# Three spaced value pairs a chunk by seven products, in a form with the signs turned, and turned tiles in four shared buffers

## The chip, the cores and the metric

The kernel runs on one core of one Trainium2 chip. The metric is the time of one execution in device microseconds (us); lower is better. The engines are PE (TensorE: matmuls), DVE (VectorE), ACT (ScalarE), POOL (GpSimd) and SP (SyncE, which here only issues transfers).

## The reference

The input is a batch of 8 with 8 heads of 1024 tokens and a head width of 64. Keys and values are projected along the sequence from 1024 to 64 rows, then attention runs over these 64, and its output goes through a gated feed-forward layer.

```python
k_proj = np.einsum('ks,bhsd->bhkd', E, k)
v_proj = np.einsum('ks,bhsd->bhkd', F, v)
scores = scale * np.matmul(q, k_proj.transpose(0, 1, 3, 2))
scores = scores - np.max(scores, axis=-1, keepdims=True)
attn = np.exp(scores)
attn = attn / (np.sum(attn, axis=-1, keepdims=True) + 1e-09)
attn_out = np.matmul(attn, v_proj)
x = attn_out.transpose(0, 2, 1, 3).reshape(B * S, H * D)      # 8192 x 512
g = x @ w_gate                                                # 512 x 1536
silu = g * (1.0 / (1.0 + np.exp(-g)))
val = x @ w_val                                               # 512 x 1536
out = silu * val @ w_out                                      # 8192 x 512
```

## The kernel before

All matmuls take bf16 inputs and sum in fp32 in PSUM. The work is cut into 16 chunks of 512 tokens, two a batch: chunk c is half c % 2 of batch c // 2. A chunk's feed-forward part has 12 blocks f of 128 columns of the hidden layer. Time is counted in steps t = 12 c + f, and every step has two slots, 2t and 2t + 1, for pieces of attention.

One step of the main loop issues, in this order: the gate matmuls of block f (`f_g`, four matmuls of 512 columns, then SiLU on ACT), the attention pieces of slot 2t, the value matmuls (`f_v`, four matmuls, then the product with the SiLU on DVE into `hT`), the list `late[t]`, and the pieces of slot 2t + 1. Everything is issued in the written order, and each engine works through its own queue in that order; semaphores hold an instruction until its inputs are there and its output buffer is free.

`late` holds the rest. `f_m(c, n)` is the output product of the chunk before. It is a 2 x 2 block product by seven products instead of eight (n runs over 14 pieces of six matmuls of 256 columns; `m_34`, `m_52`, `m_16` and `m_7` read the sums out of PSUM on ACT, POOL and DVE). `h_sum` makes the sums of quarters of `hT` that it needs: m = 1, 6, 7 on DVE in blocks 1 to 3 of the next chunk, m = 2, 5 on POOL, block by block.

The same idea is used for some value blocks. `PAIRED` says which: blocks 8 and 9 in chunks 3 to 14, blocks 10 and 11 in chunks 2 to 14. The two blocks of a pair, halved in the contraction and in the tokens, are a 2 x 2 product; seven products of two matmuls of 256 columns each take the place of two blocks of four matmuls of 512. `p_w` makes the sums of weights once, `p_x` the sums of a chunk's `xT` (67, 1, 3, 4), on POOL in even chunks and on DVE in odd ones. `f_v_pair` runs the products into two PSUM banks and puts the four outputs together on DVE.

The attention of batch b runs while the two chunks of batch b - 1 are in the feed-forward part; `place(b)` puts its pieces into slots, counted from s0 = 48 (b - 1): `u_KV` (projections; slot 8), `u_KT` (turns the projected keys, four casts by DVE into `BD`; slot 11), `u_S` (scores and exponential; slots 13, 13, 15, 15 in the even chunk, 25, 25, 27, 27 in the odd one), `u_R` and `u_N` (softmax sum with reciprocal on DVE, product on POOL), `u_AD` (SP turns the attention weights by a transposing DMA), `u_PVt` (values; four casts by ACT into `xT`). `u_TD` turns q by the same kind of DMA.

PSUM has eight banks: two for gates, two for values (`vps`, taken in turn), two for the output product, two for attention. The turned tiles (`qTd`, `AAd`, `AT`) have two buffers each.

Of the kernel before, what the change touches and what calls it, by code (L numbers as in the profile page):

```python
# [16 lines left out]
H = 8  # L17
# [21 lines left out]
PAIRED = {8: range(3, NC - 1), 10: range(2, NC - 1)}  # L39
# [4 lines left out]
def kernel(  # L44
# [34 lines left out]
    ps_v = ctx.enter_context(tc.tile_pool(name="psv", bufs=2, space=bass.MemoryType.PSUM))  # L79
# [18 lines left out]
    wo = w_pool.tile([P, NFT, DM], BF16, name="wo")  # L98
    ws = {m: w_pool.tile([P, HF, HC], BF16, name=f"ws{m}") for m in (1, 3, 4, 6, 7)}
# [57 lines left out]
    banks = {"a": (ps_a, "pa"), "g": (ps_g, "gps"), "v": (ps_v, "vps"), "y": (ps_y, "yp0"), "z": (ps_y, "yp1")}  # L157
    ring = {"n": 0, "wide": True}

    def bank(where, shape, dt, name):  # L160
        if where == "a" and ring["wide"]:
            where = "aaz"[ring["n"] % 3]
            ring["n"] += 1
        pool, tag = banks[where]
        return pool.tile(shape, dt, name=name, tag=tag)
# [179 lines left out]
    def u_TD(b, ch):  # L345

        t = aw.tile([P, 2 * H, P], BF16, name="qTd", tag="qTd")
        nc.sync.dma_start_transpose(
            out=t[:], in_=qb[b, ch][:].rearrange("p h j d -> p (h j d)")
        )  # L350
        qT[b, ch, "d"] = t

    def u_AD(b, ch):
        t = aw.tile([P, 4, NPAIR, P], BF16, name="AT", tag="AT")
        nc.sync.dma_start_transpose(
            out=t[:].rearrange("p j a t -> p (j a) t"),
            in_=AA.pop((b, ch, "d"))[:].rearrange("p j h k -> p (j h k)"),
        )
        AT[b, ch] = t
# [45 lines left out]
    def u_N(b, u, eng=nc.gpsimd):  # L405
        ch, w = divmod(u, 4)
        g, i = divmod(w, 2)
        if (b, ch) in by_dma:
            if (b, ch, "d") not in AA:
                AA[b, ch, "d"] = aw.tile([P, 4, H, KP], BF16, name="AAd", tag="AAd")  # L410
            a = AA[b, ch, "d"][:, 2 * i : 2 * i + 2, 4 * g : 4 * g + 4, :]
        else:
            a = AA[b, u] = first_batch("a", [P, 2, 4, KP], "AA")
            a = a[:]
        zr, r = rr.pop((b, u))
        eng.tensor_tensor(  # L416
            out=a.rearrange("p j h k -> p h j k"),
            in0=ee.pop((b, u))[:],
            in1=r.unsqueeze(3).to_broadcast([P, 4, 2, KP]),
            op=ALU.mult,  # L420
        )
        if maxed:
            return
        unwatched.append(zr)
        if b or u > 3:
            u_Z()
# [8 lines left out]
    def u_A(b, u, eng=nc.vector):  # L435
        ch, w = divmod(u, 4)
        g, i = divmod(w, 2)
        if (b, ch) not in AT:
            AT[b, ch] = aw.tile([P, 4, NPAIR, P], BF16, name="AT", tag="AT")
        ps = bank("a", [P, 2, 2, P], BF16, "aTp")  # L440
        a = AA.pop((b, u))
        for pr in range(2):
            for j in range(2):
                nc.tensor.transpose(
                    out=ps[:, j, pr, :],
                    in_=a[:, j, 2 * pr : 2 * pr + 2, :].rearrange("p h k -> p (h k)"),
                    identity=ident_bf[:],
                )
        copy(eng, AT[b, ch][:, 2 * i : 2 * i + 2, 2 * g : 2 * g + 2, :], ps[:])
# [88 lines left out]
    def paired(c, f):  # L538
        return not maxed and c in PAIRED.get(f - f % 2, ())

    def f_g(c, f, i=None):
        ps = f_mm(c, f, 0, i)
        if paired(c, f):
            if f % 2 == 0:
                pool, tag = {8: (q_pool, "q01"), 10: (fw, "thp")}[f]
                gp["p"] = pool.tile([P, 2, CW], FP32, name="thp", tag=tag, bufs=1)
            nc.scalar.activation(out=gp["p"][:, f % 2], in_=ps[:], func=AF.Silu)  # L547
            return
# [10 lines left out]
    def p_tiles():  # L559


        a = q_pool.tile([P, 8, HT], BF16, name="xsa", tag="q00", bufs=1)
        rows = [quarter(wo, 0, 1)[:, i] for i in range(4)] + [quarter(wo, 1, 0)[:, i] for i in range(HF)]
        for m, x in ((6, a[:, 0:2]), (7, a[:, 2:4]), (67, a[:, 0:4]), (1, a[:, 4:6]), (3, a[:, 6:8])):
            sums["x", m] = x
        sums["x", 4] = quarter(wo, 0, 1)[:, 4:6]
        for i, m in enumerate((1, 2, 5, 6, 7)):
            for n, f in enumerate((8, 10)):
                sums["w", m, f] = rows[5 * n + i].rearrange("p (k t) -> p k t", k=2)

    def p_w(m, f):

        p = f
        f = [slice(i * P, (i + 1) * P) for i in (p, p + 1)]
        a = {(i, j): wv[:, 2 * j : 2 * j + 2, f[i]] for i in range(2) for j in range(2)}
        x, y, op = {
            1: ((0, 0), (1, 1), ALU.add),
            2: ((1, 0), (1, 1), ALU.add),
            5: ((0, 0), (0, 1), ALU.add),
            6: ((1, 0), (0, 0), ALU.subtract),  # L580
            7: ((0, 1), (1, 1), ALU.subtract),
        }[m]
        nc.vector.tensor_tensor(out=sums["w", m, p], in0=a[x], in1=a[y], op=op)

    def p_x(c, m, eng):

        if not sums:
            p_tiles()
        x = xT[divmod(c, CH)]
# [3 lines left out]
            1: (b[0, 0], b[1, 1], ALU.add),  # L593
            3: (b[0, 1], b[1, 1], ALU.subtract),
            4: (b[1, 0], b[0, 0], ALU.subtract),
        }[m]
        eng.tensor_tensor(out=sums["x", m], in0=i0, in1=i1, op=op)  # L597

    def p_mm(c, p, m, ps, start=False):
# [4 lines left out]
        xs = {2: x[:, 0:2, 0:HT], 5: x[:, 2:4, HT:CW]}[m] if m in (2, 5) else sums["x", m]  # L604
# [10 lines left out]
    def f_v_pair(c, f):  # L615

        tensor_tensor = nc.vector.tensor_tensor
        p = f - f % 2
        if f == p:
            xp = gp["x"] = bank("v", [P, 2, HT], FP32, "vps")  # L620
            t = gp["t"] = fw.tile([P, 2, HT], FP32, name="vt", tag="s1", bufs=1)
            p_mm(c, p, 3, xp[:, 0], start=True)
            p_mm(c, p, 4, xp[:, 1])
            copy(nc.scalar if (c + f // 2) % 2 else nc.vector, t[:, 0], xp[:, 0])
            tensor_tensor(out=t[:, 0], in0=t[:, 0], in1=xp[:, 1], op=ALU.add)
            zp = gp["z"] = bank("v", [P, 2, HT], FP32, "vps")
            p_mm(c, p, 1, zp[:, 0], start=True)
            tensor_tensor(out=t[:, 1], in0=t[:, 0], in1=zp[:, 0], op=ALU.add)
            return
        th, xp, zp, t = (gp.pop(i) for i in "pxzt")  # L630
        th = th[:].rearrange("p i t -> p (i t)")
        h = hT[c][:, p : p + 2, :].rearrange("p i t -> p (i t)")
        p_mm(c, p, 5, xp[:, 0])
        p_mm(c, p, 2, xp[:, 1])
        tensor_tensor(out=t[:], in0=t[:], in1=xp[:], op=ALU.subtract)
        tensor_tensor(
            out=h[:, HT : 3 * HT], in0=th[:, HT : 3 * HT], in1=xp[:].rearrange("p i t -> p (i t)"), op=ALU.mult
        )
        p_mm(c, p, 6, zp[:, 1])
        p_mm(c, p, 7, zp[:, 0])  # L640
        tensor_tensor(out=t[:], in0=t[:], in1=zp[:], op=ALU.add)
        h, th = (a.rearrange("p (i t) -> p i t", i=4)[:, 0::3] for a in (h, th))
        tensor_tensor(out=h, in0=th, in1=t[:], op=ALU.mult)

    def f_v(c, f, i=None):
        if paired(c, f):
            return f_v_pair(c, f)
# [55 lines left out]
    def h_sum(c, m, f0, f1, eng=nc.gpsimd):  # L703

        if f0 == 0:
            if c == NC - 1 and m in (1, 6, 7):

                pool, tag = {1: (kv_pool, "vb"), 6: (kv_pool, "kb"), 7: (aw, "AAd")}[m]
                hs[c, m] = pool.tile([P, HF, HT], BF16, name=f"hs{m}", tag=tag)
# [125 lines left out]
    def put(s, fn, *a):  # L835
        slots[s].append((fn, a))

    def place(b):
# [11 lines left out]
        else:  # L850
# [8 lines left out]
            put(s0 + 28, u_AD, b, 0)  # L859
            put(s0 + 38, u_AD, b, 1)  # L860
            put(s0 + 44, u_PVt, b, 0, (0, 1), ("aa", "yz"))
        for j in range(NJ):
            put(sa[j], u_S, b, j)
            at = sa[j] + 1 if b == 1 else s0 + (
                (16, 17, 20, 21) if b == 2 else (14, 15, 17, 23)) [j] if j < 4 else s0 + (26, 28, 33, 35)[j - 4]
# [55 lines left out]
    with tc.manual_schedule():  # L921

        kb[0] = kv_pool.tile([P, H, NJ, D], BF16, name="kb", tag="kb")
        kraw = [aw.tile([P, 2, NJ * D], FP32, name="kraw", tag=tag) for tag in ("qTd", "AAd")]
# [148 lines left out]
        for c in range(1, NC):  # L1073
            for f in range(HF):
                for m in (5, 2):
                    at = {2: 10, 3: 11, 4: NFT, 5: NFT}[f] if paired(c, HF + f) else HF + f
                    late[c * NFT + at].append((h_sum, c, m, f, f + 1))
            if c == NC - 1:
                late[c * NFT + HF].append((h_sum, c, 6, 0, HF, nc.vector))
# [9 lines left out]
        for p, at in ((10, (3, 3, 3, 4, 4)), (8, (4, 4, 7, 7, 7))):  # L1089
            for i, f in zip((1, 2, 5, 6, 7), at):  # L1090
                late[2 * NFT + f].append((p_w, i, p))
        for c in PAIRED[10]:
            for i, m in enumerate((67, 1, 3, 4) if c % 2 == 0 else (3, 4, 1, 67)):
                f, eng = ((2, 3, 3, 5)[i], nc.gpsimd) if c % 2 == 0 else (6 + i // 2, nc.vector)
                late[c * NFT + f].append((p_x, c, m, eng))
# [3 lines left out]
        for t in range(NIT):  # L1099
# [3 lines left out]
            f_g(c, f, i)  # L1103
            run_slot(2 * t)
# [38 lines left out]
```

## Time and profile before

| | us |
|---|---|
| median of 3 runs | 544.71 (544.64 to 544.86) |
| profiled execution | 544.77 |
| its span | 543.1 |
| PE busy | 534.0 (98%) |
| DVE busy | 406.6 (75%) |
| POOL busy | 362.7 (67%) |
| ACT busy | 265.9 (49%) |
| two steady chunks (350.81 to 415.06) | 64.25, PE busy throughout |

Busy time of PE is modelled at the matmuls' ends, so it says that PE has no gaps, not that it works at its peak. The granted clock is 0.999 of full speed. A step of a steady chunk takes between 2.4 and 4 us on PE, by the attention pieces in it. The chain that ended last, followed back from the end, shows what set the time; a group's line may be that of a helper (L168 is `copy`).

### The profile page before, as it was taken

The page shows a single profiled execution, that of the slowest core. Times are in us where ns is not written, and L with a number is a line of the kernel's source. Part 1 is how long each engine was busy: PE and PEld are TensorE (multiplying, and loading weights), DVE is VectorE, ACT ScalarE, POOL GpSimd, SP SyncE. Part 2 cuts the span into 40 slices and gives each one's busy share as a digit, 9 for nine tenths or more (in the row PEclk, how much of TensorE's full clock was granted, in tenths as well). Part 3 has the DMA queues.
Part 4 walks back from the last instruction along what each step waited for, and adds up shares of the span by engine and source line. Part 5 has one row for each costly group of instructions (what it writes and reads, how often), then busy time and mean ns, then how long its engine had stood idle before and what let it go on. Part 6 is the DMA issues. An engine that isn't in the chain of part 4 may idle for free.

```text
span 543.1 us, 9860 instructions
## 1 busy us (share of the span) xinstructions
PE 534.0 (98%) x3708; PEld 328.3 (60%) x3708; DVE 406.6 (75%) x692; ACT 265.9 (49%) x454; POOL 362.7 (67%) x456
## 2 busy tenths in 40 slices
PE   8999999999999999999999999999999999999996
PEld 4654445565656666576665756566665766656665
DVE  3787897868768887689776897778975887757553
ACT  3565454564446634466335554465444663443331
POOL 6962398578466795669675694856956686565272
PEclk9999999999999999999999999999999999999999
DMA  9999969929941499007991099512992023100103
GB/s 200 191 196 200 162 145 192 180 63 150 198 96 41 98 214 192 8 34 132 215 158 40 3 198 185 122 40 63 190 185 69 39 80 78 40 39 4 43 34 121
DMA packets 112228, 62.94 MB, mean 116 GB/s; under 512 B 65968, under 2 KB 103856, under 8 KB 112176
## 3 DMA queue, kind: packets, MB, share of 16 engines
q0 software_dynamic: 43952, 29.49, 38.2%
q1 hardware_dynamic: 67392, 31.46, 25.9%
q10 hardware_dynamic: 832, 1.31, 0.8%
q8 instruction: 30, 0.49, 0.4%
q14 instruction: 22, 0.18, 0.1%
HBM read 60.29 MB, written 16.78 MB: 142 GB/s over the span
## 4 chain that ended last, share of the span: by engine, by line
PE 93%; DMA 2%; ACT 2%; POOL 1%; DVE 1%; issue 1%; POOLq 0%; ACTq 0%; DVEq 0%
PE gps L529 30%; PE yps L737 25%; PE vps L529 23%; PE vps L606 7%; PE sc L371 2%; DMA wv<-in_moe_w_val_dram 2%; PE kvp L180 2%; PE yps L671 2%; PE pv L475 1%; POOL vb L121 0%; ACT ee L379 0%; ACT xT L484 0%; POOL qb L133 0%; ACT L554 0%; ACT ysb L761 0%
## 5 line engine op out<-in xcount | busy, mean ns | idle before, releaser
L529 PE MATMUL gps<-xT,wg 128*128 128x512 bf16 (+1 forms) x772 | 196.6, 377 | 0.0
L529 PE MATMUL vps<-xT,wv 128*128 128x512 bf16 (+1 forms) x576 | 146.3, 377 | 1.1 <-DMA wv<-in_moe_w_val_dram 0.9
L720 POOL TENSOR_TENSOR hs<-hT 128x256 bf16<-128x256 bf16 x180 | 124.2, 718 | 23.1 <-DVE hT L653 21.8
L554 ACT ACTIVATE th<-gps 128x512 f32<-128x512 f32 x106 | 63.3, 597 | 136.4 <-PE gps L529 129.5
L529 PEld LDWEIGHTS <-wg 128*128 128x128 bf16 x776 | 74.0, 98 | 51.7 <-issue 0.5
L653 DVE TENSOR_TENSOR hT<-th,vps 128x512 bf16<-128x512 f32 x106 | 71.9, 679 | 43.1 <-PE vps L529 39.9
L737 PEld LDWEIGHTS <-hs 128*128 128x128 bf16 x900 | 87.9, 98 | 24.7 <-issue 0.6
L767 POOL TENSOR_TENSOR tt<-tt,ysb 128x512 f32<-128x512 f32 x28 | 35.6, 1271 | 91.0 <-DVE tt L766 90.5
L529 PEld LDWEIGHTS <-wv 128*128 128x128 bf16 x576 | 55.0, 98 | 67.1 <-issue 3.8
L416 POOL TENSOR_TENSOR AAd<-ee,zr 128x512 bf16<-128x512 f32 x56 | 59.9, 1070 | 30.1 <-ACT ee L379 17.8
L737 PE MATMUL yps<-ws,hs 128*128 128x256 bf16 x540 | 68.6, 273 | 0.2 <-DVE ysb L806 0.2
L720 DVE TENSOR_TENSOR hs<-hT 128x1536 bf16<-128x1536 bf16 (+1 forms) x49 | 65.1, 1334 | 0.1
L401 DVE TENSOR_REDUCE zr<-ee 128x8 f32<-128x512 f32 x64 | 43.3, 677 | 11.5 <-ACT ee L379 11.5
L737 PE MATMUL yps<-ws,hT 128*128 128x256 bf16 x360 | 48.8, 273 | 0.0
L737 PE MATMUL yps<-wo,hs 128*128 128x256 bf16 x360 | 48.6, 273 | 0.1
L737 PEld LDWEIGHTS <-hT 128*128 128x128 bf16 x360 | 35.2, 98 | 16.0
L547 ACT ACTIVATE thp<-gps 128x512 f32<-128x512 f32 x50 | 29.5, 597 | 31.2 <-PE gps L529 31.1
L597 POOL TENSOR_TENSOR xsa<-xT 128x512 bf16<-128x512 bf16 (+1 forms) x21 | 40.4, 1951 | 0.0
L379 ACT ACTIVATE ee<-sc 128x512 f32<-128x512 f32 x64 | 35.7, 607 | 4.3 <-PE sc L371 2.9
L756 POOL TENSOR_TENSOR tt<-xs 128x256 f32<-128x256 f32 x30 | 24.7, 824 | 16.5 <-ACT xs L754 16.5
L761 ACT COPY ysb<-yps 128x512 f32<-128x512 f32 x30 | 17.6, 585 | 27.0 <-PE yps L737 26.3
L754 ACT COPY xs<-yps 128x512 f32<-128x512 f32 x30 | 17.7, 590 | 25.3 <-PE yps L737 24.1
(133 smaller groups left out, 677.9 us busy)
## 6 DMA issues: line engine op xcount, KB each, us to landing
out_dram<-ysb SPq DMA_DIRECT2D x27, 512.0 KB, 2.8
qb<-in_q_dram POOLq DMA_DIRECT2D x14, 512.0 KB, 16.7
kb<-in_k_dram POOLq DMA_DIRECT2D x7, 1024.0 KB, 11.2
vb<-in_v_dram POOLq DMA_DIRECT2D x7, 1024.0 KB, 13.4
wo<-in_moe_w_out_dram POOLq DMA_DIRECT2D x2, 768.0 KB, 21.3
out_dram<-ysb SPq DMA_DIRECT2D x6, 256.0 KB, 2.4
kraw<-in_k_dram ACTq DMA_DIRECT2D x2, 512.0 KB, 4.7
qb<-in_q_dram POOLq DMA_DIRECT2D x4, 256.0 KB, 8.0
```

Source lines behind the costliest of these rows:

```text
L379: nc.scalar.activation(out=e[:].rearrange("p h j k -> p (h j k)"), in_=ps[:].rearrange("p a k -> p (a k)"), func=AF.Exp, scale=scale,)
L401: nc.vector.reduce_sum(out=z, in_=e[:], axis=AX.X)
L416: eng.tensor_tensor(out=a.rearrange("p j h k -> p h j k"), in0=ee.pop((b, u))[:], in1=r.unsqueeze(3).to_broadcast([P, 4, 2, KP]), op=ALU.mult,
L529: nc.tensor.matmul(out=ps[:, ts], lhsT=(wg, wv)[w][:, kt, f * P : (f + 1) * P], rhs=x[:, kt, ts], start=(kt == 0), stop=(kt == NKT - 1),)
L547: nc.scalar.activation(out=gp["p"][:, f % 2], in_=ps[:], func=AF.Silu)
L554: nc.scalar.activation(out=th[:], in_=ps[:], func=AF.Silu)
L597: eng.tensor_tensor(out=sums["x", m], in0=i0, in1=i1, op=op)
L606: nc.tensor.matmul(out=ps, lhsT=w[:, kt], rhs=xs[:, kt], start=(start and kt == 0), stop=(kt == 1), skip_group_check=True,)
L653: nc.vector.tensor_tensor(out=hT[c][:, f, :], in0=th[:], in1=ps[:], op=ALU.mult)
L720: eng.tensor_tensor(out=hs[c, m][:, fs, :], in0=quarter(hT[c], *a)[:, fs], in1=quarter(hT[c], *b)[:, fs], op=op,)
L737: nc.tensor.matmul(out=ps, lhsT=lhsT, rhs=ws[m][:, f, :] if rhs is None else rhs, start=(start and f == 0), stop=(f == HF - 1), skip_group ...
L767: nc.gpsimd.tensor_tensor(out=t[:], in0=t[:], in1=yo[c, p][:, 1:3], op=ALU.subtract)
```

## The change

Pairs are now blocks 2 and 3 (chunks 4 to 15), 5 and 6 (3 to 15), 8 and 9 (3 to 14); a plain block stands between them (blocks 4, 7, 10). The seven products are written with other signs, in four steps spread over three blocks: `p_34` and `p_1` in the first block, `p_52` in the second, `p_76` ahead of the value matmuls of the third. Products 4, 3, then 5, 2, then 7, 6 go to one PSUM bank, M1 to the other, and each bank has a name of its own (`v` takes the next one, `w` the other). ACT copies products 4 and 3 and M1 out of PSUM; DVE sums with the bank and multiplies with the SiLU in a separate step (`p_sum`, `p_h`), both inputs of `p_h` in SBUF. The SiLU of a pair's first block is issued behind that copy. M1 is added last.

All `p_x` sums are on DVE, in two sets of buffers by the parity of the chunk, and are made ahead: for an odd chunk in blocks 5 and 9 of the even chunk before, for an even one in block 11 of the chunk before and in block 0. There are five more sums of weights.

`qTd`, `AAd`, `AT` (and the first loads of k) share four rotating buffers. The slots of `u_AD` go from 28 and 38 to 29 and 42, those of `u_R` and `u_N` from 14, 15, 17, 23, 26, 28, 33, 35 to 16, 18, 20, 22, 31, 33, 36, 38 (b > 2). The POOL sums of `hT` stand at other steps.

```diff
-PAIRED = {8: range(3, NC - 1), 10: range(2, NC - 1)}
+PAIRED = {2: range(4, NC), 5: range(3, NC), 8: range(3, NC - 1)}
...
-    ps_v = ctx.enter_context(tc.tile_pool(name="psv", bufs=2, space=bass.MemoryType.PSUM))
+    ps_v = ctx.enter_context(tc.tile_pool(name="psv", bufs=1, space=bass.MemoryType.PSUM))
...
+        if where == "v":
+            v_turn[0] ^= 1
         pool, tag = banks[where]
+        if where in "vw":
+            tag += str(v_turn[0] ^ (where == "w"))
...
-        t = aw.tile([P, 2 * H, P], BF16, name="qTd", tag="qTd")
+        t = aw.tile([P, 2 * H, P], BF16, name="qTd", tag="turned", bufs=4)
...
-        t = aw.tile([P, 4, NPAIR, P], BF16, name="AT", tag="AT")
+        t = aw.tile([P, 4, NPAIR, P], BF16, name="AT", tag="turned", bufs=4)
...
-                AA[b, ch, "d"] = aw.tile([P, 4, H, KP], BF16, name="AAd", tag="AAd")
+                AA[b, ch, "d"] = aw.tile([P, 4, H, KP], BF16, name="AAd", tag="turned", bufs=4)
...
+    def paired(c, f):
+        p = 3 * ((f + 1) // 3) - 1
+        return p if not maxed and c in PAIRED.get(p, ()) and f < p + 2 else None
 
     def f_g(c, f, i=None):
         ps = f_mm(c, f, 0, i)
+        p = paired(c, f)
+        if p is not None:
+            if f == p:
+                gp["g"] = ps
+            else:
+                nc.scalar.activation(out=gp["p"][:, 1], in_=ps[:], func=AF.Silu)
             return
...
+    def p_sum(out, a, b, op):
+        nc.vector.tensor_tensor(out=out, in0=a.unsqueeze(1).to_broadcast([P, 2, HT]), in1=b, op=op)
+
+    def p_h(c, p, part, v):
+        h, th = (
+            a.rearrange("p i t -> p (i t)").rearrange("p (i t) -> p i t", i=4)[:, part]
+            for a in (hT[c][:, p : p + 2, :], gp["p"][:])
+        )
+        nc.vector.tensor_tensor(out=h, in0=th, in1=v, op=ALU.mult)
+
+    def p_34(c, p):
+        x = gp["x"] = bank("v", [P, 2, HT], FP32, "vps")
+        gp["m"] = bank("w", [P, 2, HT], FP32, "vps")
+        p_mm(c, p, 4, x[:, 0], start=True)
+        p_mm(c, p, 3, x[:, 1])
...
+        nc.scalar.copy(out=sx[:], in_=x[:])
+        gp["p"] = fw.tile([P, 2, CW], FP32, name="thp", tag="thp", bufs=1)
+        nc.scalar.activation(out=gp["p"][:, 0], in_=gp.pop("g")[:], func=AF.Silu)
+        nc.vector.tensor_tensor(out=ts[:, 0], in0=sx[:, 0], in1=sx[:, 1], op=ALU.add)
+
+    def p_1(c, p):
+        m = gp.pop("m")
+        p_mm(c, p, 1, m[:, 0], start=True)
+        nc.scalar.copy(out=gp["ts"][:, 1], in_=m[:, 0])
+
+    def p_52(c, p):
+        x, sx = gp["x"], gp["sx"]
+        p_mm(c, p, 5, x[:, 0])
+        p_mm(c, p, 2, x[:, 1])
+        p_sum(sx[:], gp["ts"][:, 0], x[:], ALU.subtract)
+        p_h(c, p, slice(1, 3), sx[:])
+
+    def p_76(c, p):
+        x, sx = gp.pop("x"), gp.pop("sx")
+        p_mm(c, p, 7, x[:, 0])
+        p_mm(c, p, 6, x[:, 1])
+        p_sum(sx[:], gp.pop("ts")[:, 1], x[:], ALU.add)
+        p_h(c, p, slice(0, 4, 3), sx[:])
+        gp.pop("p")
...
-            put(s0 + 28, u_AD, b, 0)
-            put(s0 + 38, u_AD, b, 1)
+            put(s0 + 29, u_AD, b, 0)
+            put(s0 + 42, u_AD, b, 1)
...
-                (16, 17, 20, 21) if b == 2 else (14, 15, 17, 23)) [j] if j < 4 else s0 + (26, 28, 33, 35)[j - 4]
+                16, 17 + (b > 2), 20, 22, 31, 33, 36, 38)[j]
...
-                    at = {2: 10, 3: 11, 4: NFT, 5: NFT}[f] if paired(c, HF + f) else HF + f
+                    at = (8, 7, 11, 11, 10, 11)[f] if c > 2 else HF + f
...
-        for p, at in ((10, (3, 3, 3, 4, 4)), (8, (4, 4, 7, 7, 7))):
-            for i, f in zip((1, 2, 5, 6, 7), at):
-                late[2 * NFT + f].append((p_w, i, p))
-        for c in PAIRED[10]:
-            for i, m in enumerate((67, 1, 3, 4) if c % 2 == 0 else (3, 4, 1, 67)):
-                f, eng = ((2, 3, 3, 5)[i], nc.gpsimd) if c % 2 == 0 else (6 + i // 2, nc.vector)
-                late[c * NFT + f].append((p_x, c, m, eng))
+        for p, ts in ((5, (26, 27, 28, 28, 28)), (8, (29, 29, 31, 31, 31)), (2, (42, 42, 43, 43, 43))):
+            for m, t in zip((1, 2, 5, 6, 7), ts):
+                late[t].append((p_w, m, p))
+        for c in range(3, NC):
+            for i, m in enumerate((4, 3, 1, 67)):
+                if c == 3:
+                    t = c * NFT + (2, 2, 3, 3)[i]
+                elif c % 2:
+                    t = c * NFT - (7, 7, 3, 3)[i]
+                else:
+                    t = c * NFT + (-1, -1, 0, 0)[i]
+                late[t].append((p_x, c, m))
+        for p, cs in PAIRED.items():
+            for c in cs:
+                late[c * NFT + p].append((p_1, c, p))
...
             f_g(c, f, i)
+            if "x" in gp and paired(c, f) is None:
+                p_76(c, f - 2)
             run_slot(2 * t)
             f_v(c, f, i)
```

## The prediction

> **What bounds the kernel now.** I read the page first (busy shares, then the chain that ended last), then the chain itself in order of time, and last the timelines of PE and VectorE in one steady chunk. The busy shares and the chain name the bound:
>
> ```profile
> span 543.1 us, 9860 instructions
> PE 534.0 (98%) x3708; PEld 328.3 (60%) x3708; DVE 406.6 (75%) x692; ACT 265.9 (49%) x454; POOL 362.7 (67%) x456
> ...
> PE 93%; DMA 2%; ACT 2%; POOL 1%; DVE 1%; issue 1%; POOLq 0%; ACTq 0%; DVEq 0%
> ```
>
> TensorE is the path. After the start the only PE waits in the list of waits are two of 0.2 us. So a matmul column that goes is won, any wait put in front of PE is lost, and another engine costs nothing until PE meets it. The span is 543.1 us, the profiled execution 544.77; the 1.67 outside stay. I sum against 544.77; the median of the three runs, 544.71, is 0.06 lower.
>
> Prices on PE come from the chain in order of time (start, us, what):
>
> ```profile
> 366.23 0.87 PE vps L606 x8
> 369.27 1.31 PE yps L737 x12
> ...
> 379.50 0.86 PE vps L529 x4
> ```
>
> A plain block (four matmuls of 512 columns) is 0.865 us, a matmul of 256 columns 0.109.
>
> The place that matters is in the even chunks of batches 3 to 7: the key transpose (kTp) and, one block later, the scores (sc). PE first, in the chain, then VectorE in its timeline (start, us, engine, line, what):
>
> ```profile
> 357.32 0.12 PE kTp L279 x4
> 357.44 0.86 PE gps L529 x4
> 358.30 0.86 PE vps L529 x4
> 359.17 0.65 PE yps L737 x6
> 359.82 0.54 PE sc L371 x8
> ...
> 362.74 0.45 PE sc L371 x8
> ```
> ```profile
> 357.42 0.69 DVE L772 TENSOR_TENSOR ysb<-tt,yps 128x512 f32<-128x512 f32 x1
> 358.02 0.41 DVE L291 CAST BD<-kTp 64x256 bf16<-64x256 f32 x1
> 358.44 0.42 DVE L292 CAST BD<-kTp 64x256 bf16<-64x256 f32 x1
> 358.89 0.42 DVE L291 CAST BD<-kTp 64x256 bf16<-64x256 f32 x1
> 359.33 0.43 DVE L292 CAST BD<-kTp 64x256 bf16<-64x256 f32 x1
> ```
>
> (The chain counts a piece from the end before it, 0.16 later than the matmul's start; the timeline has kTp at 357.16 and sc at 359.65.) The first eight score matmuls take 0.54 us, the next eight 0.45: the second already waits 0.09 us for the last cast of BD, which ends at 359.76. There is no slack left here.
>
> **The gain.** A pair by seven products is 14 x 0.109 = 1.53 us, two plain blocks 2 x 0.865 = 1.73: 0.20 a pair. Pairs go from 12 + 13 = 25 to 12 + 13 + 12 = 37; 12 more save 2.45 us. Weight loads (98 ns) stay under 109 ns. With nothing else: 544.77 - 2.45 = 542.3, and since PE has no other idle time to lose, this is the floor.
>
> **Even chunks, block 5 (chunks 4, 6, 8, 10, 12).** The order of the changed program there is, on PE: p_34, six output products, p_1, key transpose, gate matmuls of block 6, p_52, six output products, scores. On VectorE: ts sum, m_7, two p_x sums for the next chunk, four casts of BD. Count from the start of the key transpose. PE reaches the second score matmul at 0.11 + 0.865 + 4 x 0.109 + 0.655 + 0.055 = 2.12; before it was 2.55, as four half-width matmuls replace a plain block. VectorE: the ts sum waits for ScalarE's copy of p_34 (p_34 ends at -0.88, 0.17 matmul tail, 0.58 copy) and runs from -0.07 to 0.30; m_7 (0.60 to the next start, as 357.42 to 358.02 shows) to 0.90; the two p_x, 0.36 and 0.45, to 1.71; the casts 4 x 0.435 to 3.45. The score matmul starts at 3.50: a wait of 3.50 - 2.12 = 1.38 us, in five chunks 6.9 us. Even with free p_x sums 0.57 would be left. Price of p_x: VectorE rows give 0.42 to 0.80 for the 512-wide sum and 0.43 for the other, so the wait lies between 1.2 and 1.8; I take the low price, because POOL, whose work slowed such rows, is idle there. In the kernel before, these sums stood in blocks 6 and 7 of their own chunk, or on POOL. Queued behind the casts are p_sum and p_h of block 6, and p_76 on PE waits for that p_sum; it comes at 4.2, PE needs it at 4.9, so no second wait.
>
> **Odd chunks, blocks 2 to 7 (chunks 5, 7, 9, 11, 13).** The softmax sums (L401 + L402, 0.85 us) now stand in blocks 3, 4, 6 and 7, between the pairs' steps. Count from the end of p_34 of block 2. PE runs p_1, products and gates and asks for p_76 of pair 5 at 11.3 (block 3 ends at 2.83, block 4 at 6.30, block 5 at 8.48, block 6 at 10.43, gates of block 7 0.865). That p_76 overwrites the bank that p_sum of block 6 reads. VectorE up to there: p_h of block 3 waits for its SiLU, and ScalarE has to do 0.75 to the end of the copy, the 1.28 table load (L547 shows it), two SiLUs and a small copy: 3.5. Then p_h 0.6, DVE hs sum 1.2, softmax 0.85, p_sum 0.72, p_h 0.6, plain product 0.6, m_16 0.42: 8.5. m_7 needs POOL's subtraction after m_16 (0.14 + 1.27): 9.95; m_7 0.6, softmax 0.85, p_sum 0.7: 12.1. PE waits 12.15 - 11.3 = 0.85 us; five chunks 4.3 us. Without POOL's wait it is 0.5; the rows below bound it above.
>
> **The two-input rows.** New are 74 p_h and 37 ts sums with both inputs in SBUF. The nearest row is L643, 25 of them: shortest 691 ns, median 693, longest 1120, mean 895, so nearly half are long, those where POOL works on hT sums or on L767. I use 0.69 (0.6 to the next start), because POOL's only work near the odd chunk's walk is one softmax product and L767. At 1.12 two of them in the odd chunk add 0.86: a wait of up to 1.7 there, 8.5 in all. The other way, seven chunks' p_x leave POOL (25.9 + 14.8 + 8.1 = 48.8 us of it), which frees VectorE.
>
> The Trainium skill, page "SBUF — State Buffer", section "Who interferes with whom", says that a VectorE instruction with two SBUF inputs contends with a GpSimd instruction that reads SBUF, and one with a single SBUF input does not. The 691 and 1120 ns of L643 fit it, and it speaks against this form, in which twice as many products a pair read both inputs from SBUF; taken for one p_h in each odd chunk it would make the total 2.2 us longer by my estimate.
>
> **Other engines and queues.** VectorE in all: pairs cost 25 x about 4.0 us before (0.42 + 0.42 + 0.42 + 3 x 0.68 + 0.69), 37 x 3.2 to 3.6 after (0.42 + 2 x 0.68 + 2 x 0.69 to 0.9), 24 plain products of 0.68 go, about 16 us of p_x and 3 of p_w come: 428 to 443 us, still under PE. ScalarE gains 37 x (0.58 + 0.37) - 13 x 0.37 = 30 us, and the SiLU of a pair's first block is now behind a copy and in two places a table load: it ends 2.63 after p_34, while the gates two blocks on want its bank at 2.83. Covered by 0.15; if that goes, up to 0.3 in ten chunks. SP: the AT transposes move from slots 28 and 38 to 29 and 42; they land in 8.8 us and are used 15 and 14 slots later, near 20 us. The four shared buffers: each new tile takes the one released four tiles before, and in this order (q, q, A, T, A, T) that reader is done; the closest is the second q turn, which waits in SP for the value matmuls of the same slot, with one output store behind it. I take zero for both; were a transpose late it would cost up to its 8.8 us once a batch, which nothing here suggests. Chunks 2 and 3, the one with 5 more weight sums (0.58 each) and its sums in its own blocks: 0 to 1 us, taken as 0.
>
> **Sum:** 544.77 - 2.45 + 6.9 + 4.3 = 553.5 us.
>
> **Rivals.**
> Both waits (the forecast): 551 to 556, chance 0.45.
> Only the cast is late, and the odd chunk's VectorE queue keeps pace (its ends are 0.5 to 0.85 late in my walk, and a SiLU half a microsecond earlier would do): 544.77 - 2.45 + 6.9 = 549.2, 0.19.
> Both waits and POOL's contention on p_h and on the hs sums (DVE L720 runs from 1.0 to 2.2 us): 556 to 560, 0.11.
> Half of it, should VectorE run the small sums closer than I think: 545.9 to 548, 0.07.
> Same, 0.03.
> The other side: no wait is exposed, 542.3, 0.15. It needs the casts to end within 2.1 us of the key transpose; for it speaks that VectorE is busy 24.7 of 32.1 us in such a chunk, so there is room somewhere; against it that m_7 and the casts alone take 2.34 from a start that is not before 0.26. It decides at 0.49 us of wait a chunk: below that in these five chunks, with quiet odd ones, the change gains.
> That fewer products are run than written is no case: the built program has 37 x 14.
>
> **Range and chances.** From the half case to the contended one, 545.5 to 558: left out are the 0.15 and 0.03 below and a little above. 0.2% of this kernel, 1.1 us, is what a measurement can tell. Faster 0.15, same 0.03, slower 0.82.
>
> **What would show it.** Right: PE sc waiting for DVE BD five times, near 1.4 us each; PE vps (p_76) waiting for DVE sx near block 7 of odd chunks; score matmuls starting about 3.5 us after the key transpose; 518 half-width value matmuls; POOL busy down by some 45 us. Wrong: no PE wait over 0.3 us, and a chain that is all PE, or waits at ScalarE's SiLU or at SP's transposes in their place.

## The result, and the profile after

The changed kernel takes 565.78 us (median of six runs, 564.77 to 566.03), the kernel before 544.72 (six runs, 544.51 to 545.23): 1.0383 times as long, interval 1.037 to 1.0396. The forecast was 553.5, so the direction was right and 12.3 us were missing. Five of the six executions of the changed kernel, with a granted clock of 0.997, took 565.59 to 566.03 us, the sixth, at 1.000, 564.77. All values below are from a profiled execution of 566.03 us, 21.3 above the profiled one of before.

The page first: span, busy shares, and the shares of the chain that ended last.

```profile
span 564.5 us, 9975 instructions
...
PE 532.3 (94%) x3712; PEld 336.1 (60%) x3780; DVE 429.3 (76%) x724; ACT 289.6 (51%) x515; POOL 324.2 (57%) x428
...
PE 74%; DVE 15%; issue 5%; POOL 3%; DMA 2%; ACT 2%; DVEq 0%; ACTq 0%; POOLq 0%
```

PE does slightly less (534.0 before) in a longer span, and its share of the chain falls from 93% to 74%. VectorE has 23 us more work and is only 76% busy, but now holds 15% of the chain: it is late in certain places, not full. The list of waits says where (engine, what waited, for what: us in total, times, longest):

```profile
PE yps L762 <- DVE tt L791: 10.5, 11, 1.0
PE sc L378 <- DVE BD L299: 4.5, 10, 0.7
PE vps L616 <- DVE sx L627: 2.4, 2, 2.1
PE bad L907 <- DVE sane L903: 2.2, 1, 2.2
```

Only the second of these lines was forecast as it stands. The third is the kind of wait that was forecast (`p_76`), but both of its entries stand in chunk 3 and none in the odd chunks from 5 on. The first, the largest, is an output product (`f_m`) that waits for `m_16` (L791; L766 in the kernel before).

**The scores (even chunks).** The chain in order of time (start, us, what), from the key transpose to the scores:

```profile
302.10 0.13 PE kTp L286 x4
...
302.82 0.42 DVE x L607
303.24 0.33 DVE xsa L607
303.57 0.33 DVE BD L298
...
304.80 0.44 DVE BD L299
...
305.28 0.55 PE sc L378 x7
```

The two `p_x` sums (L607) stand ahead of the four casts, and the last cast lets the scores go. In PE's timeline the transpose starts at 301.94, so the second score matmul starts 3.34 us after it (forecast 3.50). The first score matmul is 0.38 us late and the second 0.84 more, 1.22 a batch, five times.

**The output products.** PE's timeline (start, us, what, and in brackets the idle time before and its releaser), first block 11 of the even chunk, then block 5 of the odd one:

```profile
317.40 1.03 PE L536 MATMUL vps<-xT,wv 128*128 128x512 bf16 x4
319.47 0.82 PE L762 MATMUL yps<-ws,hs 128*128 128x256 bf16 x6 [1.04 <-DVE tt L791]
...
334.46 0.38 PE L616 MATMUL vps<-xsa,wv 128*128 128x256 bf16 x2
335.76 0.81 PE L762 MATMUL yps<-ws,hs 128*128 128x256 bf16 x6 [0.92 <-DVE tt L791]
```

The durations overlap; the due time is the start before it plus the prices of the prediction. Four matmuls of 0.865 from 317.40 make 318.27, and the product starts at 319.47: 1.20 late. Two of 0.109 from 334.46 make 334.68, and it starts at 335.76: 1.08 late. This product writes the half bank that `m_16` reads for the piece before, so it can't start until `m_16` has read it. VectorE's timeline for the same two places:

```profile
314.48 1.88 DVE L607 TENSOR_TENSOR xsa<-xT 128x512 bf16<-128x512 bf16 x2
...
319.00 0.41 DVE L791 TENSOR_TENSOR tt<-tt,yps 128x256 f32<-128x256 f32 x1
...
325.87 0.69 DVE L681 SCALAR_TENSOR_TENSOR s<-th,gps 128x512 f32<-128x512 f32 x1 [3.07 <-ACT th L560]
...
335.30 0.41 DVE L791 TENSOR_TENSOR tt<-tt,yps 128x256 f32<-128x256 f32 x1
```

In the even chunk two `p_x` sums, which take 1.88 us beside a softmax product of POOL, stand ahead of `m_16`. In the odd one VectorE idles 3.07 us until 325.87, then works with hardly a gap up to `m_16`: a burst. What it waits for until then is a tanh on ScalarE (L560), which stands there behind a table load of 1.28 us and two exponentials of 1.08; no run moved it.

**Chunk 3 and the flag, once each.** The timelines of VectorE, POOL and PE around `p_76` of the first pair:

```profile
131.93 3.19 DVE L647 TENSOR_TENSOR ts<-sx 128x256 f32<-128x256 f32 x1
...
131.60 0.94 POOL L135 DMA_DIRECT2D qb<-in_q_dram  x1
132.56 1.28 POOL L792 TENSOR_TENSOR tt<-tt,ysb 128x512 f32<-128x512 f32 x1
133.78 1.05 POOL L423 TENSOR_TENSOR AAd<-ee,zr 128x512 bf16<-128x512 f32 x1
...
137.16 0.38 PE L616 MATMUL vps<-xsa,wo 128*128 128x256 bf16 x2 [2.07 <-DVE sx L627]
```

A `ts` sum, 413 ns at its shortest, takes 3.19 us while POOL goes from one piece of work to the next, and `p_76` is 2.23 late. Late in the program a flag that guards the softmax's range (`u_sum`, `u_flag`, in slots 38 and 40 of the last batch) holds PE for 2.3 us: its sum waits for POOL's part of the last softmax piece, which has moved from slot 35 to slot 38. The chain there:

```profile
477.51 1.04 POOL AAd L423
...
478.97 0.17 DVE sane L903
...
479.18 0.19 PE bad L907 x2
```

Soon after this wait PE works at half speed for 3.3 us: up to 483.5 a matmul of 256 columns takes 0.21 us instead of 0.109. The view by stretches shows it (stretch, its length, busy time and instructions of PE, PEld, DVE, ACT and POOL; then the granted clock, the DMA share and GB/s):

```profile
480.00:484.00 4.00, 4.00 (x20) 2.35 (x18) 1.03 (x2) 2.00 (x4) 2.54 (x4) 0.57 0.52 118
```

That is 1.7 us more. One such stretch stands in the profiles of three runs below as well (`flag_later`, `px_behind_both`, `moves_without_gap`), each time begun at most 1.2 us after PE had waited 1.7 to 2.3 us; other waits as long have none behind them. What sets it off isn't shown, but it enters or leaves the times by up to 1.7 us.

| lateness of PE, start to start | us |
|---|---|
| scores, 5 x 1.22 | 6.1 |
| output product, even block 11, 5 x 1.20 | 6.0 |
| output product, odd block 5, 5 x 1.08 | 5.4 |
| `p_1` of odd chunks, 4 x 0.11 | 0.4 |
| chunk 3: 0.79 + 2.23 + 0.36 + 0.23 | 3.6 |
| flag | 2.3 |
| matmuls at half speed behind the flag | 1.7 |
| small waits of 0.08 to 0.36 that only the kernel before has | -1.6 |
| 12 more pairs x 0.204 | -2.45 |
| sum | 21.5 |

The difference of the two profiled executions is 21.3.

### The profile page after: what moved, and what is told of

Its sections match the earlier page's. It is cut to its first block, busy times and chain, and to the rows that moved or that the text cites. A ratio compares the mean times of both kernels' runs of the same rounds, so it can differ in the third digit from the quotient of the medians.

```text
span 564.5 us, 9975 instructions
## 1 busy us (share of the span) xinstructions
PE 532.3 (94%) x3712; PEld 336.1 (60%) x3780; DVE 429.3 (76%) x724; ACT 289.6 (51%) x515; POOL 324.2 (57%) x428
## 3 DMA queue, kind: packets, MB, share of 16 engines
q10 hardware_dynamic: 832, 1.31, 0.8%
## 4 chain that ended last, share of the span: by engine, by line
PE 74%; DVE 15%; issue 5%; POOL 3%; DMA 2%; ACT 2%; DVEq 0%; ACTq 0%; POOLq 0%
PE gps L536 22%; PE yps L762 19%; PE vps L536 16%; PE vps L616 8%; DMA wv<-in_moe_w_val_dram 2%; PE kvp L187 2%; PE sc L378 2%; DVE hs L745 2%; PE yps L696 2%; DVE sx L627 2%; DVE ts L647 1%; PE pv L482 1%; DVE hT L678 1%; DVE hT L634 1%; DVE zr L408 1%
## 5 line engine op out<-in xcount | busy, mean ns | idle before, releaser
L536 PE MATMUL vps<-xT,wv 128*128 128x512 bf16 (+1 forms) x459 | 118.9, 376 | 1.4 <-DMA wv<-in_moe_w_val_dram 0.8
L563 ACT ACTIVATE th<-gps 128x512 f32<-128x512 f32 x82 | 49.0, 597 | 95.2 <-PE gps L536 86.9
L536 PEld LDWEIGHTS <-wv 128*128 128x128 bf16 x480 | 45.2, 98 | 50.9 <-issue 6.5
L678 DVE TENSOR_TENSOR hT<-th,vps 128x512 bf16<-128x512 f32 x82 | 55.4, 676 | 26.1 <-PE vps L536 22.0
L634 DVE TENSOR_TENSOR hT<-thp,sx 128x512 bf16<-128x512 f32 x74 | 56.8, 767 | 6.8 <-ACT thp L556 2.2
L627 DVE TENSOR_TENSOR sx<-ts,vps 128x512 f32<-128x512 f32 x74 | 50.1, 677 | 15.0 <-PE vps L616 12.8
L745 DVE TENSOR_TENSOR hs<-hT 128x1536 bf16<-128x1536 bf16 (+1 forms) x49 | 48.2, 989 | 0.0
L644 ACT COPY sx<-vps 128x512 f32<-128x512 f32 x37 | 21.7, 586 | 51.4 <-PE vps L616 50.8
L681 DVE SCALAR_TENSOR_TENSOR s<-th,gps 128x512 f32<-128x512 f32 x35 | 23.6, 673 | 21.6 <-ACT th L560 20.8
L647 DVE TENSOR_TENSOR ts<-sx 128x256 f32<-128x256 f32 x37 | 27.0, 729 | 16.7 <-ACT sx L644 16.2
```

Source lines behind the costliest of these rows:

```text
L536: nc.tensor.matmul(out=ps[:, ts], lhsT=(wg, wv)[w][:, kt, f * P : (f + 1) * P], rhs=x[:, kt, ts], start=(kt == 0), stop=(kt == NKT - 1),)
L563: nc.scalar.activation(out=th[:], in_=ps[:], func=AF.Silu)
L627: nc.vector.tensor_tensor(out=out, in0=a.unsqueeze(1).to_broadcast([P, 2, HT]), in1=b, op=op)
L634: nc.vector.tensor_tensor(out=h, in0=th, in1=v, op=ALU.mult)
L647: nc.vector.tensor_tensor(out=ts[:, 0], in0=sx[:, 0], in1=sx[:, 1], op=ALU.add)
L678: nc.vector.tensor_tensor(out=hT[c][:, f, :], in0=th[:], in1=ps[:], op=ALU.mult)
```

## The experiments

Three theories were set against each other. *Queue order*: some instructions stand at wrong places in VectorE's queue, and moving them gives the loss back at the same amount of work. *Too much work*: 37 pairs load VectorE too densely, so that a wait removed appears again elsewhere. *Contention*: instructions with two inputs in SBUF last longer beside POOL. Every run was timed beside the kernel before, the ratios are to it, and the diffs are against the changed kernel unless said.

**The `p_x` sums behind the casts.**

```diff
-                    t = c * NFT - (7, 7, 3, 3)[i]
+                    t = c * NFT - (6, 6, 3, 3)[i]
```

> The first two p_x sums for an odd chunk stand in block 6 of the even chunk before, behind the casts of BD, instead of in block 5 ahead of them. Queue order (VectorE reaches at a fixed handful of places what PE waits for too late, and each place is paid for by itself): the casts end 0.67 us earlier (302.82 to 303.49 in the trace of the changed kernel), so the scores' wait goes from 1.22 to about 0.55 in five chunks, 3.3 us less: 562.4. Too much work (the new form gives VectorE more than its queue can place, so time taken off one wait comes back at the next): less than 1.5 us won, the rest appears at m_16 or p_76. Contention (VectorE instructions with two SBUF inputs held up by POOL are the loss): no change within 0.5 us, as nothing is taken off POOL.

562.67 us, 1.0331 (1.0314 to 1.0348). The scores' lateness falls from 1.22 to 0.55 a batch; the prediction had put what is left without these sums at 0.57. The output products stay late (1.31 and 1.08).

**The last output product a block later.** The fourteen pieces are spread otherwise, so that `m_16` has more time.

```diff
-                for n, f in enumerate((0, 1, 2, 3, 4, 4, 5, 6, 7, 8, 9, 10, 10, 11)):
+                for n, f in enumerate((0, 1, 2, 3, 4, 4, 6, 6, 7, 8, 9, 10, 10, 12 if c < NC - 2 else 11)):
```

> Each last output product of a half, the one that writes the bank that m_16 reads, is issued a block later (block 6 instead of 5, block 0 of the next chunk instead of 11; chunk 15 keeps its order). Queue order: the waits for m_16 (1.08 and 1.20 us in each of five batches, 0.8 in chunk 3) go, and the scores come 0.65 later with m_7 behind the casts, so 1.0 of their 1.22 goes too; in the odd chunks p_76 of pair 5 then meets its p_sum about 0.5 late: about 565.8 - 5 x 2.8 - 0.8 = 551. Too much work: the waits move on to p_76 and to the value banks, under 6 us won, 560 or more. Contention: 564 to 566.

560.96 us, 1.0293 (1.0273 to 1.0314): a miss by some 10 us. The waits for `m_16` are gone from the list, but PE now waits for the value banks:

```profile
PE vps L616 <- DVE hT L678: 5.8, 11, 0.9
PE vps L616 <- DVE sx L627: 3.6, 7, 1.8
```

They are freed by VectorE too: the wait moved to other matmuls. Here *too much work* told more than *queue order*.

**The softmax slots of before.** Pieces of work that VectorE had at other steps before.

```diff
-                16, 17 + (b > 2), 20, 22, 31, 33, 36, 38)[j]
+                (16, 17, 20, 21) if b == 2 else (14, 15, 17, 23)) [j] if j < 4 else s0 + (26, 28, 33, 35)[j - 4]
```

> The slots of the softmax sums and products are those of the kernel before (14, 15, 17, 23, 26, 28, 33, 35). Queue order: in odd chunks one softmax sum less stands ahead of m_16 (0.85 us), in even chunks too, so the two waits at the output product go from 1.08 and 1.20 to about 0.3 each in five batches, 8.4 us, and the flag's product no longer waits 2.3 us for the last softmax product: about 555. Too much work: the sums come back in the way of p_34 and p_52 in odd blocks 1 and 2, less than 4 us won. Contention: 563 to 566.

560.1 us, 1.0276 (1.0259 to 1.0293). The lateness at `m_16` falls to 0.67 and 0.20, and the flag's wait is gone. But `p_76` of the odd chunks' first pair is now 1.78 late; from the list of waits:

```profile
PE vps L616 <- DVE sx L627: 8.1, 6, 1.6
```

So about half of what was looked for. The softmax sums load the odd chunk's burst, but in their old slots they stand ahead of `p_sum` there, and two of VectorE's `hT` sums, there beside other work of POOL, last 1.73 and 1.79 us (0.95 in the changed kernel).

**The flag later.**

```diff
-        for s, fn in ((38, u_sum), (40, u_flag), (88, u_bad)):
+        for s, fn in ((44, u_sum), (46, u_flag), (88, u_bad)):
```

> The sum of the watch values and the flag's product stand at slots 44 and 46 of the last batch's odd chunk instead of 38 and 40. Queue order: PE's single wait of 2.3 us for VectorE, which waits for POOL's last softmax product there, goes: 563.5. Too much work: VectorE loses the same time in the next blocks, under 1 us won. Contention: no change within 0.5 us.

562.8 us, 1.0323 (1.0303 to 1.0344), and the wait is gone: the loss of 2.3 is order alone. (In this profile the half-speed stretch stands behind the wait of 2.23 in chunk 3.)

**One input of the `ts` sum from PSUM.** Same sum, same place, but one of its inputs is read where the matmul left it.

```diff
-        nc.vector.tensor_tensor(out=ts[:, 0], in0=sx[:, 0], in1=sx[:, 1], op=ALU.add)
+        nc.vector.tensor_tensor(out=ts[:, 0], in0=sx[:, 0], in1=x[:, 1], op=ALU.add)
```

> The ts sum takes product 3 from its PSUM bank instead of from the copy, so it has one SBUF input instead of two; the wait of p_52 for that bank now includes the sum. Contention (VectorE instructions with two SBUF inputs are held up by POOL, and that is a part of the loss): all 37 ts sums last about 0.42 us instead of up to 3.2 (mean 0.73), the 2.2 us wait of p_76 in chunk 3, which follows the longest of them, goes, and the odd chunks' wait for m_16 shrinks by up to 0.5 in five batches: 561 to 563.5. Queue order alone or too much work: ts is short of no input, its length is work, and nothing changes within 1 us; in odd block 2, where ts stands behind an hs sum, p_52 may wait up to 0.3 a batch longer.

562.98 us, 1.0328 (1.031 to 1.0345). The line's own entry, of the changed kernel and then of this one (times, ns shortest/median/longest, first and last start):

```profile
L647 DVE TENSOR_TENSOR ts<-sx x37: 413/617/3191, 131.9 to 535.2; 128x256 f32<-128x256 f32 x37
```
```profile
L647 DVE TENSOR_TENSOR ts<-sx,vps x37: 368/420/423, 131.8 to 531.9; 128x256 f32<-128x256 f32 x37
```

Beside the same work of POOL in chunk 3 it takes 0.37 us where it took 3.19, and `p_76` there is 1.07 late for 2.23. So *contention* is shown. But in chunk 3 the time gained comes back at two matmuls behind, which are now 0.81 late (0.36 in the changed kernel) and 0.92 late (in time there). PE's timeline of this run:

```profile
140.62 0.38 PE L616 MATMUL vps<-xsa,wo 128*128 128x256 bf16 x2 [0.65 <-DVE hT L678]
142.61 0.60 PE L616 MATMUL vps<-xT,wo 128*128 128x256 bf16 x4 [0.75 <-DVE ts L647]
```

Chunk 3 loses 3.6 us in all, as before. What goes is 1.6 us of small waits in the other chunks (even block 11 is 1.07 late for 1.20, odd block 5 1.00 for 1.08, `p_1` in time). The time fell by 2.8, as *contention* gave it, but not by this alone: this profile has no half-speed stretch, which is about the rest.

**The `hT` sums of VectorE into the idle 3 us.**

```diff
-                    late[(c + 1) * NFT + 1 + i].append((h_sum, c, m, 0, HF, nc.vector))
+                    late[(c + 1) * NFT + ((0, 0, 1)[i] if c % 2 == 0 and c > 1 else 1 + i)].append((h_sum, c, m, 0, HF, nc.vector))
```

> In odd chunks from 3 on the three hT sums on VectorE stand in blocks 0, 0 and 1 instead of 1, 2 and 3, where the trace has VectorE idle for 3.07 us before the tanh. Queue order: m_16 in odd block 4 no longer has one of them in its burst and comes about 1 us sooner, so the 1.08 us wait goes to under 0.2 in five batches and the one of 0.8 in chunk 3 too: 565.8 - 5.5 = 560.3, and the even chunks stay as they are. Too much work: the waits move to p_52, p_76 or the banks, under 2 us won. Contention: the sums at block 0 collide with POOL's hT sums and get slower; 565 to 567.

565.41 us, 1.0374 (1.0357 to 1.0391): a miss. The lateness at the odd `m_16` does halve (1.08 to 0.54), but the sums now run beside POOL's own `hT` sums. Six of these take 5.41 us in POOL's timeline from 323.72 (3.81 in the changed kernel, from 323.49), and PE is 1.26 us late at them in each of five chunks. The row of POOL's timeline, then the list of PE's waits:

```profile
323.72 5.41 POOL L745 TENSOR_TENSOR hs<-hT 128x256 bf16<-128x256 bf16 x6
...
PE yps L762 <- POOL hs L745: 5.5, 5, 1.1
```

VectorE's idle gap was not free to use, because POOL was busy in it.

**The `p_x` sums behind the casts and behind `m_16`.**

```diff
-                    t = c * NFT - (7, 7, 3, 3)[i]
+                    t = c * NFT - (6, 6, 2, 2)[i]
```

> The p_x sums for an odd chunk stand in blocks 6 and 10 of the even one before instead of 5 and 9: behind the casts of BD and behind m_16. Queue order: beside the 3.3 us at the casts, m_16 in even block 10 comes by the 1.9 us sooner that the two sums take in block 9, and its wait of 1.20 us in five batches goes: 565.8 - 3.3 - 6.0 = 556.5. Too much work: the second 6 us come back in odd blocks 0 to 5, 560 to 562. Contention: as one or the other, since the sums last 1.9 and not 0.85 us by POOL's softmax product beside them; in block 10 they would last 0.9 to 1.5.

557.41 us, 1.0224 (1.0199 to 1.0249), close to what *queue order* gave. The wait of the even block 11 is gone, and the sums take 1.27 us in block 10 where they took 1.88 in block 9. The scores stay 0.55 late and the odd `m_16` 1.25. With the same instructions and the same pairs, 8.4 us come back.

**Five moves together**: this one, the `hT` sums in the gap, the flag, `ts` from PSUM, and the key transpose a slot earlier:

```diff
-            put(s0 + (13 if b == 2 else 11), u_KT, b)
+            put(s0 + (13 if b == 2 else 10), u_KT, b)
```

> Five moves at once, all products kept: p_x in blocks 6 and 10, the hT sums of odd chunks in blocks 0, 0 and 1, the key transpose at slot 10 (ahead of p_34, where VectorE is idle 1.43 us) instead of 11, the flag at 44 and 46, ts with one SBUF input. Queue order: every wait that the trace of the changed kernel shows after 94 us goes (18.0 in five batches, 3.8 in chunk 3, 2.3 at the flag), and what is left is the product count: 542.5 to 545, level with the kernel before or just below. Too much work: at least 5 us of waits come back in other places, 549 or more. Contention: the hT sums and p_h still meet POOL, 550 or more.

553.16 us, 1.0147 (1.013 to 1.0164): a miss by about 10 us. The scores are in time; what is left is mostly the wait that the gap made, 1.45 a batch, and 0.36 at `m_16`:

```profile
PE yps L762 <- POOL hs L745: 6.7, 5, 1.6
```

**The kernel before with the four shared buffers alone.** Against the kernel before; only tags change, as here (and for `AT`, `AAd`, the first loads of k and the seventh `hT` sum):

```diff
-        t = aw.tile([P, 2 * H, P], BF16, name="qTd", tag="qTd")
+        t = aw.tile([P, 2 * H, P], BF16, name="qTd", tag="turned", bufs=4)
```

> The kernel before with one part of the change alone: qTd, AAd, AT and the first loads of k in four shared rotating buffers, its own slots kept. All theories: each tile takes over from one whose reader is done, so no wait is added: 544.7, within 0.3 us. If SP's transposes had to wait for a buffer, PE would show waits for turned tiles and the time would rise by 1 us or more.

545.03 us, 1.0003 (0.9994 to 1.0013). The buffers cost nothing that can be measured.

**One pair a chunk**, blocks 8 and 9 alone: 12 pairs, everything else as in the changed kernel.

```diff
-PAIRED = {2: range(4, NC), 5: range(3, NC), 8: range(3, NC - 1)}
+PAIRED = {8: range(3, NC - 1)}
```

> The changed kernel with the pairs of blocks 8 and 9 alone (12 pairs), blocks 2, 3, 5 and 6 plain; all else, the places of p_x and the softmax slots too, as changed. Products: 13 pairs fewer than in the kernel before cost 2.65 us, 547.4. Queue order: p_x ahead of the casts, p_x ahead of m_16 and the flag stay, so about 0.8 at the scores and 1.2 at the output product in five batches and 2.3 at the flag stay: 559. Too much work of the new form: with a third of the pairs VectorE keeps pace, 547 to 550. Contention: 548 to 554, as p_h and ts are a third.

556.28 us, 1.021 (1.0193 to 1.0227). By count this kernel would take 542.3 + 25 x 0.204 = 547.4, so 8.9 are lost with a third of the pairs. The scores (0.77 a batch) and the even block 11 (1.20, unchanged) are still late; the odd chunks' waits and the flag's are gone, and chunk 3's are down to 0.8:

```profile
PE yps L762 <- DVE tt L791: 5.4, 6, 1.0
PE sc L378 <- DVE BD L299: 3.0, 5, 0.6
```

(5 x 1.97 and 0.8 make 10.7; less the 1.6 of small waits that only the kernel before has, 9.1.) So most of the even chunks' loss, 1.97 of 2.42 us a batch, does not come from the number of pairs. The odd chunks' does depend on it.

**The moves without the gap.** The four other moves, and instead of the gap the odd chunk's softmax sums later, past the burst:

```diff
-                16, 17 + (b > 2), 20, 22, 31, 33, 36, 38)[j]
+                16, 17 + (b > 2), 20, 22, 35, 37, 39, 41)[j]
```

> As all_five_moves, but the hT sums stay in blocks 1 to 3, and in odd chunks the softmax sums stand at slots 35, 37, 39 and 41 instead of 31, 33, 36 and 38. Queue order with contention as the runs so far show it: POOL's hT sums end in time again (1.45 us in five batches won back against all_five_moves), m_16 in odd block 4 has no softmax sum ahead of it and waits under 0.3, 0.26 at p_52 and about 2 in chunk 3 stay: 545 to 547.5. Too much work: the odd burst meets p_52 or p_76 of pair 5, 550 or more.

545.05 us, 0.9997 (0.9988 to 1.0007): with all 37 pairs and as many instructions, 20.7 of the 21.1 us are back. What is left late is `p_52` in block 6 of the even chunks, 0.26 five times, because the `ts` sum that reads its bank stands behind the casts, and 0.61 + 1.70 in chunk 3, with a half-speed stretch behind the latter.

**The same without pairs in chunk 3** (35 pairs):

```diff
-PAIRED = {2: range(4, NC), 5: range(3, NC), 8: range(3, NC - 1)}
+PAIRED = {2: range(4, NC), 5: range(4, NC), 8: range(4, NC - 1)}
```

> As moves_without_gap, and chunk 3 has no pairs (its three transfers of q and k and its own p_x sums stand in blocks 2 to 5, and its waits are 2 to 3.8 us). The two pairs cost 0.41 us. Queue order with contention: 1.5 to 2 us less than moves_without_gap, 544 to 545.5. Too much work: as moves_without_gap within 0.5, since the sums of chunk 3 stay.

542.21 us, 0.9953 (0.9936 to 0.9969), faster than both kernels. Ten pairs more than before, at 0.204, make 544.77 - 2.04 = 542.7. It is 2.8 below the run with 37 pairs, more than was expected: the 2.3 of waits in chunk 3 are gone, and so is the half-speed stretch behind them. From the page, the chain:

```profile
PE 92%; POOL 3%; DMA 2%; DVE 1%; issue 1%; POOLq 0%; DVEq 0%
```

PE has the chain again, as in the kernel before.

**What they settle.** *Queue order* explains most of the loss: moving instructions, and taking one input from PSUM, brings nearly all of it back. How much of the 20.7 us is each of the two no run shows, as the moves were not run together without the operand from PSUM; moving `p_x` alone gave 8.4. *Contention* decides which places are good (the `ts` sum, the gap that couldn't be used), and in part the two are one: the `p_x` sums of block 9 took 1.88 us and those of block 5, with POOL idle, 0.67, and at 0.67 the wait of 1.20 behind block 9 would be nearly gone with the order unchanged, an estimate from these numbers. *Too much work* is refuted as a cause of the whole, but holds inside the odd chunk's burst, where taking one wait away without moving work out only shifted it.

## Why the prediction was wrong

| term | forecast | measured |
|---|---|---|
| gain, 12 pairs | -2.45 | not apart; ten pairs, 2.04 by count, ended 2.5 below |
| scores, even chunks | 6.9 | 6.1 |
| odd chunks' wait | 4.3, at `p_76` | 5.4 at the output product, 0.4 at `p_1` |
| output product, even block 11 | not in the sum | 6.0 |
| chunks 2 and 3 | 0 | 3.6 |
| flag | not in the sum | 2.3 |
| half-speed stretch | not in the sum | 1.7 in the profiled execution |

**The step that failed** is the list of what on PE waits for VectorE in these blocks. "That p_76 overwrites the bank that p_sum of block 6 reads" was right, but the prediction did not say the same of the output product, which overwrites the half bank that `m_16` reads. Its own walk had `m_16` end 8.5 us after `p_34` of block 2; in the trace `p_34` of block 2 starts at 326.64, so it ends four matmuls later, at 327.07, and `m_16` at 335.71, 8.64 after that. By the prediction's own prices the product that waits is due at 7.60 (block 4 ends at 6.30, gates 0.865, `p_34` of block 5 0.436). So the walk held a wait of 0.9 at `m_16` already and passed over it on the way to `p_76`, which was then not late: the wait had been paid. In the odd chunks this put a size not far off (4.3 for 5.4) at a wrong place; that the two lie close is luck, as the 0.85 at `p_76` was summed from other terms than the 0.9 at `m_16`. In the even chunks it left out 6.0: only block 5 was walked, although the `p_x` sums were said to stand "in blocks 5 and 9", and block 9 is ahead of the second `m_16`.

**The scores** went as forecast in place and cause, and nearly in size. The walk gave 2.12 us for when PE reaches the second score matmul, and it is due at 304.06, 2.12 after the transpose. The casts let it go 0.16 sooner than in the walk, because the two `p_x` sums took 0.67 us there and not 0.81.

**The two-input rows.** The price of `p_h` was right: 691 ns at its shortest, median 692, longest 1151 (0.69 and 1.12 in the prediction). What it left out is that the other sums with both inputs in SBUF are held up too: the two `p_x` sums of block 9 took 1.88 us, and a `ts` sum, priced at 0.37, took 3.19. The Trainium skill, page "SBUF — State Buffer", section "Who interferes with whom", says that such an instruction contends with a GpSimd instruction that reads SBUF and that one with a single SBUF input does not; 3.19 us with both inputs in SBUF and 0.37 with one from PSUM, at the same place, agree with it. The prediction used the rule to weigh one `p_h` a chunk and not for `ts` and `p_x`, the rows that were held longest.

**Chunk 3 and the flag.** "0 to 1 us, taken as 0" was not walked; the trace has 3.6. A contended `ts` sum stands ahead of the largest of these waits, but the run that read PSUM kept the 3.6 at other matmuls. The flag's wait was not thought of: the moved softmax slots were followed to VectorE's queue, not to the last reader of their results.

**What held.** VectorE busy 429.3 (428 to 443 forecast), POOL 38.5 less (some 45), no cost of the buffers (measured), none at SP's transposes or at ScalarE's SiLU in the list of waits. The floor of 542.3 was near the truth but no floor: 35 pairs took 542.21, where the same count gives 542.7. That PE had "no other idle time to lose" left out small waits like the 0.09 to 0.10 us at the scores. The rival with "POOL's contention on p_h and on the hs sums" (556 to 560) named a real cause, but not its places; the time lay 7.8 above the end of the range.

## What to carry to other kernels

When a change makes one engine later, list every matmul that writes a bank which that engine still reads, in order of time, the ones of unchanged code too, and compare each one's due time with the reader's end; the first one to fail takes the wait, and later ones then look innocent. Walk every block that a moved instruction stands in, and every reader of what it makes, down to checks that run once. Before a change is given up for time lost at waits, try it with the same work at other places in the queue: here that, and one operand's place, gave 20.7 of 21.1 us back.

## What the runs showed of the hardware

A sum of 256 columns with both inputs in SBUF, 0.41 us at its shortest, lasted 3.19 us, past three pieces of POOL's work one after the other (a transfer's issue 0.94, a sum 1.28, a softmax product 1.05), not only for the one that had begun before it. The other way round, VectorE's `hT` sums moved beside POOL's made six of POOL's last 5.41 us where they had taken 3.81. That a neighbour can be held for several instructions had not been expected from the 0.69 and 1.12 us that the trace of before shows.

A wait of PE can cost more than itself: behind waits of 1.7 to 2.3 us four of the fourteen profiles have one stretch of 3.3 us in which matmuls take twice their time (granted clock 0.57 over the 4 us from 480 in the changed kernel), 1.7 us each. The profiles of the kernels without such long waits show none.
